# Attention, two expert layers, one kernel: another order for the last attention tiles, and all stores of x on SyncE

## The chip, the cores and the metric

One core of one Trainium2 chip. The metric is the device time of one execution in microseconds (us), and a kernel's time is the median of its runs. Engines are named as in the profile: PE (TensorE), DVE (VectorE), ACT (ScalarE), POOL (GpSimd) and SP (SyncE, which here only issues DMAs).

## The reference

Three layers, all in float32, one after the other:

```python
# q, k, v: (4, 8, 576, 64); rel = query position - key position
scores = q @ k.T / 8                       # heads 0-3 keep 0 <= rel < 32
p = softmax(mask(scores))                  # heads 4-7 keep 0 <= rel < 128, rel % 4 == 0
x = (p @ v).transpose(0, 2, 1, 3).reshape(2304, 512)

e = argmax(x @ w_gate)                     # one of 8 experts per token
s = max_softmax(x @ w_gate) * sigmoid(x @ w_output_gate)[e]
x = s * relu(x @ w1[e]) @ w2[e]            # w1: (8, 512, 1024), w2: (8, 1024, 512)

out = softplus(x @ w_in) @ w_out           # 512 -> 2048 -> 512
```

## The kernel before, in words

**Attention.** The 2304 tokens are 20 tiles, five per batch: w = 0 to 3 have 128 tokens, w = 4 has 64. Tile i is batch i // 5. A loop over i from 0 to 21 is a pipeline written out by hand: step i makes the scores and the softmax of tile i, the transposed probabilities, sums, values and the division (`normalise`, L443) of tile i - 1, and the transposed x and its copy to SBUF (`transpose_x`, `evict_x`, L497) of tile i - 2. PE, ACT, DVE and SP each run their instructions in the order in which this text gives them out; only POOL's order is made by a scheduler. Heads 0 to 3 (half 0 of x, columns 0 to 255) use V as `vP`; heads 4 to 7 (half 1) are dilated by 4, use V as `vD`, and their rows lie in the tile as 4 residues of 32 tokens: partition 32 r + m is token 4 m + r.

**Stores of x.** `normalise` writes the finished tile to `x_dram`. For tiles 0 to 13 POOL stores half 0 (L459) and, where w < 4, half 1 by an indirect DMA whose rows are listed in `xrow` (L463); for the w = 4 tiles, and for tiles 14 to 19 wholly, SP does it: one transfer for half 0 and one per residue for half 1 (L473). Behind `normalise` in SP's order stand the loads of the next batch's V (`load_v`): six transfers of three heads of vD at w = 4, earlier ones at w = 0 and 2; and q and k of the batch after that at w = 1 and 3.

**Routing.** Tiles are routed in six groups (0 to 3, 4 to 7, 8 to 10, 11 to 13, 14 to 16, 17 to 19) by a generator that is moved on one DVE instruction at a time (`pump`, or `go` in the lists below): logits on PE, a transpose of them, the argmax, a rank within the expert by small matmuls, then the place of each token. POOL scatters the places to `idx_dram`.

**The first expert's tokens.** After group 2 one expert is picked as the first (rank 0, 424 columns) and its weights are loaded. Its x is not read back token by token but gathered in four PSUM accumulators `xacc` of 128 features each. Tokens of tiles 0 to 13 are gathered by POOL (L843, four transfers of up to 128 rows) and added by matmuls with a diagonal (`mm_gathered`, L968). Tiles 14 to 19 are read back from `x_dram` (`load_late`, `ll`, L988), scaled and split in a high and a low half (`split_late`, `sp`: high on ACT L999, low on DVE L1001), and added by a matmul with a 0/1 selection (`sel_late`, `se`, L1010; `mm_late`, L1020). Tiles 14 and 19 have 64 rows each and share one such operand. Then the four accumulators are split again, high on ACT and low on DVE (`split_rank0`, L1033, L733), and the expert's matmuls begin (L900 to L902).

**What sets the order at the end of attention.** Lists of events `at(step, place, ...)`, run by `events`; what is left runs in the list `late` after the loop (L1212). At step 20 the high and low halves of tiles 15, 14 and 16 are given out before tile 19's `evict_x`; at step 21 comes one accumulator's gathered part, then the logits of tile 19.

**PSUM.** Eight banks: two for scores, one for values, five that rotate (`ps_t`) for all transposes, logits, ranks and the fourth accumulator. After attention they are given anew: two for transposes, three for the second expert matmul, three for the first.

Of the kernel before, what the change touches and what calls it, by code (L numbers as in the profile page):

```python
# [21 lines left out]
P = 128  # L22
# [20 lines left out]
def attn_moe_softplus_kernel(ctx: ExitStack, tc: tile.TileContext, q, k, v, w_gate, w_ogate, w1, w2, w_in, w_out, out, dbg=None):  # L43
# [8 lines left out]
    NW = 5  # L52
# [9 lines left out]

    x_dram = dram.tile([NT, DM], F32, name="x_dram")
    idx_dram = dram.tile([NE * NT + 512, 2], I32, name="idx_dram")
# [16 lines left out]
    tabp = const.tile([1, 1], I32, name="tabp")  # L81
    xrow = const.tile([P, NTL], I32, name="xrow")

# [38 lines left out]
    def consts2():  # L122
        nc.gpsimd.memset(upper, 1.0)
        nc.gpsimd.affine_select(upper, upper, [[1, P]], ALU.is_gt, 0.0, base=0, channel_multiplier=-1)
        nc.gpsimd.memset(ones, 1.0)
        nc.gpsimd.memset(lg, 0.0)
        nc.gpsimd.memset(cumb, 0.0)
        nc.gpsimd.iota(rev, [[-1, NE]], base=NE, channel_multiplier=0, allow_small_or_imprecise_dtypes=True)
        nc.gpsimd.iota(eidx, [[1, NE]], base=0, channel_multiplier=0, allow_small_or_imprecise_dtypes=True)
        for r in range(4):  # L130
            nc.gpsimd.iota(
                xrow[32 * r : 32 * r + 32].rearrange("p (b w) -> p b w", w=NW),
                [[2 * S, B], [2 * P, NW]], base=2 * r + 1, channel_multiplier=8,
            )

        nc.gpsimd.memset(ebase, 0.0)
        nc.gpsimd.tensor_scalar(ebase[0:1], eidx[0:1], float(NT), None, ALU.mult)
        for b in range(B):
            nc.gpsimd.iota(pair[:, NW * b : NW * b + NW, 0], [[P, NW]], base=b * S, channel_multiplier=1)
# [89 lines left out]
    ps_o = psctx.enter_context(tc.tile_pool(name="ps_o", bufs=1, space=PSUM))  # L229
    ps_t = psctx.enter_context(tc.tile_pool(name="ps_t", bufs=5, space=PSUM))  # L230

# [69 lines left out]
    def transpose_qk(b, half, ti, y):  # L301

        ps = ps_t.tile([P, 512], F32, tag="tp", name=f"pqk{b}{half}{ti}{y}")
# [133 lines left out]

    X_POOL = GROUPS[G_DRAM][1]  # L440
    x_stores = []

    def normalise(b, w):  # L443
# [12 lines left out]
        pump()  # L456
        i = NW * b + w
        eng = nc.gpsimd if i < X_POOL else nc.sync
        sts = [eng.dma_start(x_dram[t0 : t0 + nt, :256], x2[:nt, :256])]  # L459
        if i < X_POOL and w < NW - 1:  # L460

            sts.append(
                nc.gpsimd.indirect_dma_start(  # L463
                    out=x_dram.rearrange("t (h d) -> (t h) d", h=2),
                    out_offset=IndirectOffsetOnAxis(ap=xrow[:, i : i + 1], axis=0),
                    in_=x2[:, 256:],
                    in_offset=None,
                )
            )
        else:  # L470
            rows = x_dram[t0 : t0 + nt, 256:].rearrange("(m r) d -> m r d", r=4)
            for r in range(4):
                sts.append(nc.sync.dma_start(rows[:, r], x2[32 * r : 32 * r + nt // 4, 256:]))  # L473
        for k_, st in enumerate(sts):
            on_pool = i < X_POOL and (k_ == 0 or w < NW - 1)
            for e, e_pool in x_stores:
                if on_pool or e_pool:
                    tc.declare_no_dep(st.ins, e.ins, reason="no two stores of x have a row and half in common")
            x_stores.append((st, on_pool))

    def transpose_x(b, w):
        d = tl[b, w]
        x2 = d["x"].rearrange("q a h d -> q (a h d)")
        ps = ps_t.tile([P, 512], F32, tag="tp", name=f"px{b}{w}")
        for c in range(4):
# [61 lines left out]
    def route(g):  # L547
# [16 lines left out]
        cb = K["rt"].tile([P, NE], F32, tag="rcb", name=f"rcb{g}")  # L564
        posi = t2("rposi", I32)
        V.tensor_copy(lg[:, js], xT.pop(g)[:, :G4])
# [116 lines left out]
    def order():  # L683
        V = nc.vector
        pc = K["px"][0].tile([P, 512], F32, tag=K["px"][1], name="pcnt")[:, :NE]
        nc.tensor.matmul(pc, ones, cumb[:, len(GROUPS)], start=True, stop=True)

        def o3(nm):
# [4 lines left out]

        cnt, key, rank, g, r, lt, tmp, tab = o2("ocnt"), o2("okey"), o2("orank"), o3("og"), o3("or_"), o3("olt"), o3("otmp"), o2("otab", 40)
        ov = K["rt"].tile([1, NE, NT // OVW], F32, tag="oov", name="oov", bufs=1)
# [4 lines left out]
        V.memset(tab, 0.0)  # L700
        V.scalar_tensor_tensor(key, pc[0:1], float(NE), rev[0:1], ALU.mult, ALU.add)
        V.scalar_tensor_tensor(key, first[0:1], float(2 * NE * NT), key, ALU.mult, ALU.add)
        V.tensor_copy(cnt, pc[0:1])
        yield
        V.tensor_tensor(g, bce(key, NE), bc(key, NE), ALU.is_gt)
# [246 lines left out]
    def acc(c):  # L952
        pool, tag = ((ps_s, "s"), (ps_s, "s"), (ps_o, "o"), (ps_t, "tp"))[c]
        xacc[c] = pool.tile([P, 512], F32, tag=tag, name=f"xacc{c}")
# [5 lines left out]

    def mm_gathered(cs):
        for c in cs:
            if c not in xacc:
                acc0(c)
        for t in range(ntile(CAPS[0])):
            rows = min(P, CAPS[0] - P * t)
            for c in cs:
                nc.tensor.matmul(  # L968
                    xacc[c][:, P * t : P * t + rows],
                    xg[0, t][:rows, P * c : P * c + P],  # L970
                    xacc["d", t][:rows, :rows],
                    start=False,
                    stop=False,
                    skip_group_check=True,
                )

# [125 lines left out]
    at(21, 0, ("az", 0), ("az", 1))  # L1102
    at(21, 1, ("mg", 0))
    for g, (t0, t1) in enumerate(GROUPS):
# [9 lines left out]
    at(20, 2, ("sc", 0), ("sc", 1), ("sc", 2), ("sc", 3))  # L1114
    at(20, 3, ("se", 14), ("se", 15), ("sp", 15, "hl"), ("sp", 14, "h"), ("se", 16), ("sp", 16, "h"), ("ll", 18), ("ll", 19))
    at(21, 1, ("go", 5, 4), ("sp", 16, "l"), ("mg", 1), ("go", 5, 8), ("sp", 14, "l"))
    ordering = order()

    def events(i, s):
        for what, *a in EV.get((i, s), ()):  # L1120
# [12 lines left out]
            elif what == "mg":  # L1133
                mm_gathered(a)
            elif what == "ll":
# [14 lines left out]
            elif what == "sp":  # L1150
                split_late(*a)

    for i in range(n + 2):
# [55 lines left out]
    def w_lo(i, j):  # L1209
        lo_(0, j)  # L1210

    late = []  # L1212
    for c in (2, 3):
        late += [(mm_late, 15, (c,), (0,)), (mm_gathered, NL, (c,))]
    late += [(mm_late, 15, (c,), (1,)) for c in (2, 3)] + [(mm_late, 15, (c,)) for c in (0, 1)] + [(mm_late, 16, (c,)) for c in range(NC)]
    late += [(fn, i) for fn in (sel_late, split_late) for i in range(17, n)] + [(w_lo, 17, j) for j in (0, 1)]
    late += [(mm_late, 17, (c,)) for c in range(NC)]

    late += [(mm_late, i, (c,)) for i, c in ((n - 2, 0), (n - 2, 1), (n - 1, 0), (n - 1, 1), (n - 2, 2), (n - 1, 2), (n - 2, 3), (n - 1, 3))]
    while late:  # L1220
        if bg:
            pump()
        fn, i, *a = late[0]
        g = next(g for g, (t0, t1) in enumerate(GROUPS) if t0 <= i < t1)
        if fn is mm_gathered or all(e[2] != g for e in bg):
            late.pop(0)
            fn(*a) if fn is mm_gathered else fn(i, *a)
    for fn in deferred:
        fn()
    actx.close()  # L1230
# [302 lines left out]
```

## Time and profile before

| | |
|---|---|
| Median of 3 runs | 806.53 us (804.1 to 810.0) |
| Profiled execution | 803.44 us, span of its instructions 801.8 us |
| Busy: PE, DVE, ACT, POOL | 764.0, 548.5, 479.3, 119.9 us |
| Attention with its tail | to about 157 us of the span |
| Experts, then the last layer | the rest |

How to read the rows below. Times count from the start of the span. A line of a timeline gives start, duration, engine, source line, instruction, operands and how many instructions are merged (x4); in brackets stands the idle time of the engine before it and what ended that. SPq is SP's DMA issue: the time is that of the issue, not of the transfer. A DMA issue line gives a transfer's size and the median time from issue to landing. In a line of windows, 1.00 at the clock means that PE was granted its full 2.4 GHz, 0.50 means 1.2 GHz, and a value between says that the level changed within the window.

### The profile page before, as it was taken

How to read it: one execution, taken by the hardware profiler on the slowest of the kernel's cores; microseconds unless marked ns; L12 is line 12 of the kernel's file. 1: busy time of each engine (PE TensorE's matmuls, PEld its weight loads, DVE VectorE, ACT ScalarE, POOL GpSimd, SP SyncE). 2: the span in 40 equal slices, each digit the busy share in tenths (PEclk: the TensorE clock that was granted, in tenths of full speed). 3: DMA queues.
4: the chain of work that ended last, by engine and by line, in shares of the span. 5: the costliest groups of instructions: out<-in, count | busy, mean ns of one | idle time of the engine just before them, and what ended most of it. 6: DMA issues, size and time to landing. Idle time of an engine off the chain costs nothing.

```text
span 801.8 us, 15124 instructions
## 1 busy us (share of the span) xinstructions
PE 764.0 (95%) x5542; PEld 690.7 (86%) x5543; DVE 548.5 (68%) x1098; ACT 479.3 (60%) x935; POOL 119.9 (15%) x154
## 2 busy tenths in 40 slices
PE   6998886999999999999999999999999999999994
PEld 4666665898999999999989999999998999999993
DVE  6967885763667977885698877766656656656561
ACT  4776642344556666666798878655556555655551
POOL 9814343121002011100000000110000001001001
PEclk8999997799999999999999999999999999999997
DMA  9996766255789999879524211310000001001001
GB/s 236 266 248 171 147 161 150 79 184 188 239 273 292 315 304 320 294 249 306 173 80 132 78 47 41 119 40 20 1 14 27 0 1 40 1 1 40 1 1 39
DMA packets 87008, 106.60 MB, mean 133 GB/s; under 512 B 30524, under 2 KB 61500, under 8 KB 86912
## 3 DMA queue, kind: packets, MB, share of 16 engines
q1 hardware_dynamic: 75616, 86.32, 36.9%
q0 software_dynamic: 5104, 13.40, 5.2%
q10 hardware_dynamic: 6192, 5.56, 2.0%
q8 instruction: 65, 1.06, 0.6%
q14 instruction: 31, 0.25, 0.1%
HBM read 85.03 MB, written 20.37 MB: 131 GB/s over the span
## 4 chain that ended last, share of the span: by engine, by line
PE 69%; issue 8%; DVE 5%; ACT 3%; DMA 2%; POOL 0%; ACTq 0%; SPq 0%; POOLq 0%; DVEq 0%
PE pg L900 7%; PE pg L901 7%; PE pg L902 7%; PE q L1442 7%; PE q L1441 7%; PE q L1443 7%; PE py L896 3%; PE py L897 3%; PE py L898 3%; PE ph L896 3%; PE ph L898 2%; PE ph L897 2%; PE ph L900 1%; PE ph L902 1%; PE ph L901 1%
## 5 line engine op out<-in xcount | busy, mean ns | idle before, releaser
L900 PE MATMUL pg<-xhm,wh 128*128 128x384 f32 x384 | 129.5, 337 | 0.5 <-ACT l L1408 0.4
L901 PE MATMUL pg<-xlm,wh 128*128 128x384 f32 x384 | 129.6, 338 | 0.0
L902 PE MATMUL pg<-xhm,wl 128*128 128x384 f32 x384 | 129.4, 337 | 0.0
L733 DVE TENSOR_TENSOR wl<-wr,wh 128x1024 fp32r<-128x1024 f32 (+1 forms) x86 | 98.2, 1144 | 30.7 <-ACT wh L788 30.6
L1406 ACT ACTIVATE u<-pg 128x384 f32<-128x384 f32 x96 | 47.2, 492 | 116.5 <-PE pg L902 116.4
L1442 PE MATMUL q<-wl,gh 128*128 128x512 f32 x288 | 113.2, 393 | 0.0
L1441 PE MATMUL q<-wh,gh 128*128 128x512 f32 x288 | 113.0, 393 | 0.0
L1443 PE MATMUL q<-wh,gl 128*128 128x512 f32 x288 | 112.6, 391 | 0.0
L788 ACT CAST wh<-wr 128x1024 fp32r<-128x1024 f32 x74 | 77.2, 1047 | 15.1 <-ACT y L923 5.2
L1450 POOL DMA_INDIRECT out_dram<-o,perm_sb x18 | 18.1, 1004 | 435.9 <-DVE o L260 303.2
L1412 DVE TENSOR_SCALAR w<-u 128x384 f32<-128x384 f32 x68 | 24.6, 362 | 84.7 <-ACT u L1407 84.2
L900 PEld LDWEIGHTS pg<-xhm,wh 128*128 128x128 f32 x384 | 72.1, 188 | 5.0 <-ACT l L1408 1.1
L901 PEld LDWEIGHTS pg<-xlm,wh 128*128 128x128 f32 x384 | 72.0, 188 | 3.7
L902 PEld LDWEIGHTS pg<-xhm,wl 128*128 128x128 f32 x384 | 72.1, 188 | 0.0
L1414 DVE SCALAR_TENSOR_TENSOR u<-w,u 128x384 f32<-128x384 f32 x96 | 53.7, 560 | 21.6 <-ACT w L1410 19.3
L1443 PEld LDWEIGHTS q<-wh,gl 128*128 128x128 f32 x288 | 54.1, 188 | 12.3
L1441 PEld LDWEIGHTS q<-wh,gh 128*128 128x128 f32 x288 | 54.1, 188 | 8.6
L1442 PEld LDWEIGHTS q<-wl,gh 128*128 128x128 f32 x288 | 54.0, 188 | 8.2
L896 PE MATMUL ph<-xh,wh 128*128 128x392 f32 (+5 forms) x192 | 58.6, 305 | 1.6 <-ACT y L923 0.9
L1416 DVE TENSOR_TENSOR l<-l,u 128x384 f32<-128x384 f32 x96 | 53.5, 557 | 7.7 <-ACT w L1420 0.5
L896 PE MATMUL py<-hh,wh 128*128 128x312 f32 (+8 forms) x192 | 58.4, 304 | 0.0
L897 PE MATMUL py<-hl,wh 128*128 128x312 f32 (+4 forms) x192 | 57.3, 299 | 0.1
(205 smaller groups left out, 1746.3 us busy)
## 6 DMA issues: line engine op xcount, KB each, us to landing
wr<-in_moe_w_dram SPq DMA_DIRECT2D x64, 512.0 KB, 6.1
praw<-in_moe_w_out_dram SPq DMA_DIRECT2D x12, 512.0 KB, 5.8
raw<-in_q_dram SPq DMA_DIRECT2D x8, 576.0 KB, 6.9
raw<-in_k_dram SPq DMA_DIRECT2D x8, 576.0 KB
x2r<-yT_dram SPq DMA_DIRECT2D x12, 384.0 KB, 4.2
vP<-in_v_dram SPq DMA_DIRECT2D x16, 272.0 KB, 9.0
praw<-in_moe_w_in_dram SPq DMA_DIRECT2D x8, 512.0 KB
wr<-in_moe_w_in_dram SPq DMA_DIRECT2D x8, 512.0 KB, 3.3
```

The source lines that it names most:

```text
L733: e.tensor_tensor(lo, src, hi.bitcast(F32), ALU.subtract)
L788: (eng or nc.scalar.copy)(d[1], d[0])
L896: nc.tensor.matmul(ps if wide else ps[:, :cut], wh, xh if wide else xh[:, :cut], start=wide, stop=False, skip_group_check=True)
L897: nc.tensor.matmul(ps[:, :cut], wh, xl[:, :cut], start=False, stop=False, skip_group_check=True)
L900: nc.tensor.matmul(ps, wh, xh, start=(first and i == 0), stop=False)
L901: nc.tensor.matmul(ps, wh, xl, start=False, stop=False)
L902: nc.tensor.matmul(ps, wl, xh, start=False, stop=(last and i == k - 1))
L1414: nc.vector.scalar_tensor_tensor(u, w_, 1.0, u, ALU.subtract, ALU.subtract)
L1416: nc.vector.tensor_tensor(l, l, u, ALU.subtract)
L1441: nc.tensor.matmul(acc[b, t], gh[:, ts_], wh, start=(f == 0), stop=False)
L1442: nc.tensor.matmul(acc[b, t], gh[:, ts_], wl, start=False, stop=False)
L1443: nc.tensor.matmul(acc[b, t], gl[:, ts_], wh, start=False, stop=(f == NF - 1))
```

## The change

Four edits. (1) All stores of x go to SP, two transfers per tile: half 0, and half 1 with its four residues in one, by a destination seen as 4 x 32 rows. A w = 4 tile stores 128 rows of half 1, 64 of them past its own (the next tile's store follows; `x_dram` has 64 more rows at the end). `xrow` and POOL's stores go away, and with them the declarations that two stores need not wait for each other. (2) Of the five rotating banks one becomes `ps_x0`, used by the transposes of x, by two of the first batch's transposes of q and k, and at the end by the fourth accumulator. (3) The list `late` goes away. All is in the lists of step 21, and `mm_gathered` takes one gathered tile and some accumulators at a time (before: some accumulators, all four tiles). (4) The scatter of the last group (`df`), the first part of the ordering of the experts (`or`: the count matmul and three DVE instructions) and the first two weight splits (`q`) stand in the same list.

```diff
-    x_dram = dram.tile([NT, DM], F32, name="x_dram")
+    x_dram = dram.tile([NT + P - S % P, DM], F32, name="x_dram")
...
-    ps_t = psctx.enter_context(tc.tile_pool(name="ps_t", bufs=5, space=PSUM))
+    ps_x0 = psctx.enter_context(tc.tile_pool(name="ps_x0", bufs=1, space=PSUM))
+    ps_t = psctx.enter_context(tc.tile_pool(name="ps_t", bufs=4, space=PSUM))
...
-        eng = nc.gpsimd if i < X_POOL else nc.sync
-        sts = [eng.dma_start(x_dram[t0 : t0 + nt, :256], x2[:nt, :256])]
...
+        nc.sync.dma_start(x_dram[t0 : t0 + nt, :256], x2[:nt, :256])
+
+        rows = x_dram[t0 : t0 + P, 256:].rearrange("(m r) d -> r m d", r=4)
+        nc.sync.dma_start(rows, x2[:, 256:])
...
-        pool, tag = ((ps_s, "s"), (ps_s, "s"), (ps_o, "o"), (ps_t, "tp"))[c]
+        pool, tag = ((ps_s, "s"), (ps_s, "s"), (ps_o, "o"), (ps_x0, "x0"))[c]
...
-    def mm_gathered(cs):
+    def mm_gathered(t, cs):
+        rows = min(P, CAPS[0] - P * t)
...
-    at(21, 1, ("mg", 0))
...
-    at(20, 3, ("se", 14), ("se", 15), ("sp", 15, "hl"), ("sp", 14, "h"), ("se", 16), ("sp", 16, "h"), ("ll", 18), ("ll", 19))
-    at(21, 1, ("go", 5, 4), ("sp", 16, "l"), ("mg", 1), ("go", 5, 8), ("sp", 14, "l"))
+    at(20, 3, ("se", 14), ("se", 15), ("se", 16), ("ll", 18), ("ll", 19))
+    lo2, hi2 = (0, 1), (2, 3)
+    at(21, 1, ("sp", 15, "h"), ("mg", 0, lo2), ("sp", 15, "l"), ("mg", 1, lo2), ("go", 5, 3), ("ml", 15, (2,)), ("go", 5, 1))
+    at(21, 1, ("ml", 15, (3,)), ("sp", 14, "h"), ("go", 5, 8), ("ml", 15, lo2), ("mg", 2, lo2), ("go", 5, 1), ("sp", 16, "h"))
+    at(21, 1, *(("mg", t, hi2) for t in range(3)), ("go", 5, 9), ("sp", 16, "l"), ("se", 17), ("df",), ("sp", 17, "h"), ("mg", 3, (0, 1, 2, 3)))
+    at(21, 1, *(("ml", 16, (c,)) for c in range(4)), ("sp", 17, "l"), ("se", 18), *(("ml", 17, (c,)) for c in range(4)))
+    at(21, 1, ("sp", 14, "l"), ("q", 0), ("se", 19), ("sp", 18, "hl"), *(("ml", 18, (c,)) for c in range(4)))
+    at(21, 1, ("sp", 19, "hl"), ("or",), ("q", 1), *(("ml", 19, (c,)) for c in range(4)))
...
-    late = []
-    for c in (2, 3):
-        late += [(mm_late, 15, (c,), (0,)), (mm_gathered, NL, (c,))]
-    late += [(mm_late, 15, (c,), (1,)) for c in (2, 3)] + [(mm_late, 15, (c,)) for c in (0, 1)] + [(mm_late, 16, (c,)) for c in range(NC)]
-    late += [(fn, i) for fn in (sel_late, split_late) for i in range(17, n)] + [(w_lo, 17, j) for j in (0, 1)]
-    late += [(mm_late, 17, (c,)) for c in range(NC)]
```

## Rows read from the trace of the kernel before

**Rows 1.** TensorE's waits, 155 to 300 us: total us, times, longest us.

```profile
PE ph L900 <- DVE xl L733: 1.2, 1, 1.2
```

**Rows 2.** The chain of waits, 100 to 160 us: start us, us, what.

```profile
131.81 4.24 DMA xl<-x_dram
...
136.80 0.48 ACT xT L497
...
147.48 8.02 PE xacc L1020 x38
...
156.08 0.61 DVE xl L733
```

**Rows 3.** Timeline of SyncE's DMA queue, 112 to 160 us: start us, us.

```profile
129.63 2.14 SPq L473 DMA_DIRECT2D x_dram<-x  x4
131.81 0.90 SPq L988 DMA_DIRECT2D xl<-x_dram  x2
```

**Rows 4.** Groups in 131 to 157 us: busy us, mean ns | idle.

```profile
L968 PE MATMUL xacc<-diag,xg 128*128 128x128 f32 (+1 forms) x32 | 8.5, 413 | 1.7 <-DMA xg<-x_dram,idx 1.7
...
L1001 DVE SCALAR_TENSOR_TENSOR l<-xl,pair,h 128x512 fp32r<-128x512 f32 (+1 forms) x6 | 4.4, 745 | 1.5 <-ACT h L999 1.4
...
L1010 DVE TENSOR_SCALAR sel<-slots,rm 128x424 fp32r<-128x424 f32 (+1 forms) x6 | 2.4, 435 | 0.0
L733 DVE TENSOR_TENSOR wl<-wr,wh 128x1024 fp32r<-128x1024 f32 x2 | 2.4, 1222 | 0.0
L733 DVE TENSOR_TENSOR xl<-xacc,xh 128x424 fp32r<-128x424 f32 x4 | 2.3, 597 | 4.9 <-ACT xh L1033 4.9
...
L507 PE MATMUL pl<-xT,wg 128*32 128x128 f32 x8 | 1.9, 421 | 1.0 <-ACT xT L497 1.0
...
L486 PE MATMUL px<-identf,x 128*128 128x128 f32 x4 | 0.7, 286 | 0.1
```

**Rows 5.** The timeline of VectorE, 112 to 160 us: group 5's routing.

```profile
140.47 0.20 DVE L566 COPY lg<-plt 128x48 f32<-128x48 f32 x1
...
143.51 0.17 DVE L617 RECIPROCAL pair<-rs 128x3 f32<-128x3 f32 x1
```

**Rows 6.** Windows: length, busy PE PEld DVE ACT POOL, clock, DMA share, GB/s.

```profile
126.00:128.00 2.00, 0.85 (x11) 0.66 (x10) 1.80 (x11) 1.18 (x3) 1.00 (x1) 1.00 0.49 155
128.00:130.00 2.00, 2.00 (x35) 1.74 (x35) 1.31 (x9) 0.20 (x1) 1.39 (x3) 0.53 0.65 172
148.00:150.00 2.00, 2.00 (x11) 1.93 (x10) 1.51 (x3) 0.00 (x0) 0.21 (x1) 0.85 0.17 50
```

**Rows 7.** The timeline of VectorE: tiles 8, 13 and 19 normalised.

```profile
69.04 0.69 DVE L450 TENSOR_TENSOR x<-o,rc 128x512 f32<-128x512 f32 x1 [0.54 <-PE o L424]
...
99.17 0.69 DVE L450 TENSOR_TENSOR x<-o,rc 128x512 f32<-128x512 f32 x1
...
131.09 0.69 DVE L450 TENSOR_TENSOR x<-o,rc 128x512 f32<-128x512 f32 x1 [1.78 <-PE o L424]
```

**Rows 8.** The timeline of TensorE, 45 to 112 us: the dilated half's values.

```profile
78.90 0.62 PE L424 MATMUL o<-vD,pt 128*32 128x128 f32 x16
...
106.75 0.91 PE L424 MATMUL o<-vD,pt 128*32 128x128 f32 x16
```

**Rows 9.** The timeline of SyncE's DMA queue, 0 to 140 us: one V load.

```profile
66.04 0.60 SPq L284 DMA_DIRECT2D vD<-in_v_dram  x1
```

**Rows 10.** DMA issues in 20 to 160 us, KB each, median us to landing.

```profile
xl<-x_dram SPq DMA_DIRECT2D x4, 256.0 KB, 5.0
...
x_dram<-x SPq DMA_DIRECT2D x16, 32.0 KB, 2.7
```

**Rows 11.** The page: a queue (packets, MB, share), an issue (us to landing).

```profile
q1 hardware_dynamic: 75616, 86.32, 36.9%
...
vP<-in_v_dram SPq DMA_DIRECT2D x16, 272.0 KB, 9.0
```

**Rows 12.** Busy time by engine and DMA share in 72 to 80 us.

```profile
72.00:80.00 8.00, 8.00 (x160) 6.16 (x162) 5.34 (x13) 6.57 (x12) 4.43 (x5) 1.00 0.18 44
```

More of the change, by code (lines that the diff above doesn't have):

```diff
@@ L81, in attn_moe_softplus_kernel @@
     tabp = const.tile([1, 1], I32, name="tabp")
-    xrow = const.tile([P, NTL], I32, name="xrow")
     tl = {}
@@ L129, in consts2 @@
         nc.gpsimd.iota(eidx, [[1, NE]], base=0, channel_multiplier=0, allow_small_or_imprecise_dtypes=True)
[L130 to L134, printed above, removed]
         nc.gpsimd.memset(ebase, 0.0)
@@ L301, in transpose_qk @@
     def transpose_qk(b, half, ti, y):
-        ps = ps_t.tile([P, 512], F32, tag="tp", name=f"pqk{b}{half}{ti}{y}")
+        own = b == 0 and (half, ti, y) in ((0, 0, 2), (1, 0, 2))
+        ps = (ps_x0 if own else ps_t).tile([P, 512], F32, tag="x0" if own else "tp", name=f"pqk{b}{half}{ti}{y}")
         def to(t, y):
@@ L437, in sums @@
         pump()
-    X_POOL = GROUPS[G_DRAM][1]
-    x_stores = []
     def normalise(b, w):
@@ L456, in normalise @@
         pump()
-        i = NW * b + w
-        eng = nc.gpsimd if i < X_POOL else nc.sync
-        sts = [eng.dma_start(x_dram[t0 : t0 + nt, :256], x2[:nt, :256])]
[L460 to L479, printed above, removed]
+        nc.sync.dma_start(x_dram[t0 : t0 + nt, :256], x2[:nt, :256])
+        rows = x_dram[t0 : t0 + P, 256:].rearrange("(m r) d -> r m d", r=4)
+        nc.sync.dma_start(rows, x2[:, 256:])
     def transpose_x(b, w):
@@ L483, in transpose_x @@
         x2 = d["x"].rearrange("q a h d -> q (a h d)")
-        ps = ps_t.tile([P, 512], F32, tag="tp", name=f"px{b}{w}")
+        ps = ps_x0.tile([P, 512], F32, tag="x0", name=f"px{b}{w}")
         for c in range(4):
@@ L564, in route @@
         cb = K["rt"].tile([P, NE], F32, tag="rcb", name=f"rcb{g}")
-        posi = t2("rposi", I32)
+        posi = (const.tile([P, 4], I32, name="rposi_last")[:, :G4] if g == len(GROUPS) - 1 else t2("rposi", I32))
         V.tensor_copy(lg[:, js], xT.pop(g)[:, :G4])
@@ L684, in order @@
         V = nc.vector
-        pc = K["px"][0].tile([P, 512], F32, tag=K["px"][1], name="pcnt")[:, :NE]
+        pc = ps_t.tile([P, 512], F32, tag="tp", name="pcnt")[:, :NE]
         nc.tensor.matmul(pc, ones, cumb[:, len(GROUPS)], start=True, stop=True)
+        cnt, key = [const.tile([1, NE], F32, name=nm) for nm in ("ocnt", "okey")]
+        V.scalar_tensor_tensor(key, pc[0:1], float(NE), rev[0:1], ALU.mult, ALU.add)
+        V.scalar_tensor_tensor(key, first[0:1], float(2 * NE * NT), key, ALU.mult, ALU.add)
+        V.tensor_copy(cnt, pc[0:1])
+        yield
         def o3(nm):
@@ L692, in o2 @@
             return K["rt"].tile([1, n], F32, tag=nm, name=nm, bufs=1)
-        cnt, key, rank, g, r, lt, tmp, tab = o2("ocnt"), o2("okey"), o2("orank"), o3("og"), o3("or_"), o3("olt"), o3("otmp"), o2("otab", 40)
+        rank, g, r, lt, tmp, tab = o2("orank"), o3("og"), o3("or_"), o3("olt"), o3("otmp"), o2("otab", 40)
         ov = K["rt"].tile([1, NE, NT // OVW], F32, tag="oov", name="oov", bufs=1)
@@ L700, in order @@
         V.memset(tab, 0.0)
[L701 to L704, printed above, removed]
         V.tensor_tensor(g, bce(key, NE), bc(key, NE), ALU.is_gt)
@@ L964, in mm_gathered @@
                 acc0(c)
[L965 to L975, printed above, removed]
+            nc.tensor.matmul(
+                xacc[c][:, P * t : P * t + rows],
+                xg[0, t][:rows, P * c : P * c + P],
+                xacc["d", t][:rows, :rows],
+                start=False,
+                stop=False,
+                skip_group_check=True,
+            )
     def rows_of(i):
@@ L1133, in events @@
             elif what == "mg":
-                mm_gathered(a)
+                mm_gathered(*a)
+            elif what == "ml":
+                mm_late(*a)
             elif what == "ll":
@@ L1151, in events @@
                 split_late(*a)
+            elif what == "df":
+                deferred.pop()()
+            elif what == "or":
+                next(ordering)
     for i in range(n + 2):
@@ L1208, in attn_moe_softplus_kernel @@
             K["rt"] = K["rt2"]
-    def w_lo(i, j):
-        lo_(0, j)
-    late = []
-    for c in (2, 3):
-        late += [(mm_late, 15, (c,), (0,)), (mm_gathered, NL, (c,))]
-    late += [(mm_late, 15, (c,), (1,)) for c in (2, 3)] + [(mm_late, 15, (c,)) for c in (0, 1)] + [(mm_late, 16, (c,)) for c in range(NC)]
-    late += [(fn, i) for fn in (sel_late, split_late) for i in range(17, n)] + [(w_lo, 17, j) for j in (0, 1)]
-    late += [(mm_late, 17, (c,)) for c in range(NC)]
[L1219 to L1229, printed above, removed]
     actx.close()
```

## The prediction, made before the changed kernel was run

> **What bounds the kernel now.** I read the list of waits after 155 us first: TensorE waits once for the first expert matmul and hardly again [rows 1], so from there to the end the span is TensorE's work, and a microsecond saved before it is a microsecond off the span. Then the chain of waits between 131 and 157 us [rows 2], the stretch that the new tail order rewrites. The reader is to see a queue of unlike things. SyncE issues the load of tile 16's x at 131.81; it lands 4.2 us later; ScalarE makes the high half of that tile, and only then copies tile 19's transposed x (136.80). That copy had nothing to wait for: it stands behind the high half in ScalarE's order. Tile 19's logits, the last routing and everything of tiles 17 to 19 follow from it. The stretch ends with 38 accumulating matmuls in a row and the last xl split on VectorE at 156.69, for which the first expert matmul waits 1.2 us [rows 1, 2]. SyncE's queue shows why the load was late: the four half-1 stores of tile 18 stand ahead of it, 2.14 us of issue [rows 3].
>
> **The tail, part by part.** In the new order nothing of tiles 14 to 16 stands ahead of tile 19's copy. Tile 19's x is normalised at 131.8 [rows 7]; transposes 0.7 [rows 4] and copy 0.5 [rows 2] with their gaps put the logits at 133.1 instead of 137.3.
>
> VectorE from there, by the grouped rows of 131 to 157 us [rows 4]: six low halves 4.4; three of the six selections 1.2 (the other three come first, to 133.6); two weight splits 2.4; four xl splits 2.3. The routing of group 5 from its copy at 140.47 to the end of its reciprocal is 3.2, and seven small ones (two copies ahead of it, the place cast, the count's keys) at the reciprocal's 0.17 are 1.2 [rows 5]. Sum 14.7, from 133.6 to 148.3. Three times VectorE has to wait for TensorE (transposed logits, ranks, count), each behind a block of accumulating matmuls; a block of four gathered ones is 8.5 / 8 at the low clock and some 0.5 at the high one [rows 4]; three times 0.5 is 1.5, and the last xl is written at 149.8.
>
> TensorE over the same stretch: 8 logits matmuls 1.9, 32 gathered 8.5, mostly at the low clock [rows 4], so 5.2 at the high one; 38 late ones in 8.0, mostly at the high clock [rows 2]. Sum 13.1, from 133.1 to 146.2: below VectorE's 149.8, so VectorE sets the end if the clock is high. The own bank for the fourth accumulator takes away the 1.2 us wait: the expert matmuls' first bank no longer holds the accumulator that is split last. They can begin with the first split, and since four terms of three matmuls take about as long as four splits (2.3), the start in effect is some 1.7 ahead of 149.8: 148.1 against 156.7, a gain of **8.6**.
>
> The clock is the doubtful part. The granted clock was at half after a stretch in which TensorE was busy 0.85 of 2.00 us, and came back only within 148 to 150 [rows 6]. With the copy in time the one gap left near there is some 0.6 us, so I expect the high level for most of the tail. If it stays at the low one as long as before (0.85 of the level over 148 to 150 is a rise at 148.6), 15.5 us do half their work, 7.75 of 13.1, the rest ends at 154.0, the last split at 155.0, and the gain is 3.4. Bounds 3.4 and 8.6; I take **7.0**, nearer the upper, because TensorE then has nearly no idle time left there.
>
> **Loads and late tiles.** With two issues of about 0.5 each [rows 3] instead of five per tile, SyncE is out of the way 1.5 us earlier per tile; the load of tile 19 still has to wait until its store has landed, but it is used only after tile 18's halves, some 10 us after x, so it is covered. If that cover went, the exposed part would be a landing, 5.0 [rows 10]. The load also needs a free buffer, which the split of tile 15 gives at about 134.6, in time. A w = 4 tile now stores 64 rows too many, which the next tile overwrites: its half-1 store must wait for the earlier one to land. The issue behind it is a load needed 10 us later or more; costed at nothing, at most 2.7 [rows 10].
>
> **Moved from GpSimd to SyncE.** Fourteen tiles' stores leave GpSimd, which is on no link of that chain; taken as nothing. On SyncE they stand, in order, ahead of the next batch's V loads, which before were issued as soon as a buffer was free. The last six of each batch (three heads of vD) come behind the x store of the batch's fourth tile. For the second and third change that tile is normalised at 69.7 and 99.9 [rows 7]; two stores 1.0, and the sixth of six issues at 0.60 [rows 9] starts 4.0 later: 73.7, 103.9. With a landing of 5.0, the nearest row in kind (a load by SyncE in a busy stretch [rows 10]), they are there at 78.7 and 108.9; TensorE reads them at 78.9 and 106.75 [rows 8]. So the second fits by a hair, as the first does, whose code and spacing are those of the second, and the third costs 2.1. Lower bound: with the 2.7 of a small store none is late, 0. Upper bound: with 9.0, as the V loads of the first half needed, 3.8 + 3.8 + 6.1 = 13.7 [rows 11]. I take **2.1**.
>
> **PSUM and the rest.** Four rotating banks for five, with the x transposes moved out of them: no wait of TensorE in the list names such a bank, so 0; at most a bank is short once a batch by one half-clock block of transposes, 0.7 [rows 4], or 2.8 in all. Dropping the iota on GpSimd and the indirect stores: 0.
>
> **Sum.** 7.0 - 2.1 = 4.9. The profiled execution took 803.4 (span 801.8 and 1.6 around it), 3.1 under the median of 806.5; so 798.5 for such an execution, and 801.6 at the level of the median.
>
> **Rivals.** (a) **All of it comes through**: the V loads land in time and the clock stays high, 8.6 gained: 797.9. For it: the DMA engines have room just where the second batch's loads are needed [rows 12]. Against: every one of the three batches has to be in time.
>
> (b) **The order does not do what it says**: the clock stays low for the tail and the expert matmuls still wait for the last split (if a bank is held by another tile). Gain 3.4 - 1.7 = 1.7, less 2.1: 806.9. For it: before, the clock came back only in the late block, at 148 or after [rows 2, 6].
>
> (c) **Slower, the V loads behind the x stores**: TensorE waits at the first vD matmuls of tiles 5, 10 and 15 by the upper bound, 13.7, and the tail gives 7.0: 813.2. It decides from a landing of about 6.7 us on: there the waits are 1.5 + 1.5 + 3.8 = 6.8 and take nearly all that the tail gives. For it: the V loads are the longest to land in the page [rows 11]. Against: the engines were busy only 0.18 of 72 to 80 us, just where the second batch is needed [rows 12].
>
> (d) **Few queues for half 1.** Its destination is written as 4 x 32 x 256, so the outermost count is 4. If only four of the sixteen queues carried it, each would serve 32 packets of 1 KB in place of 8; at 62.6 ns a packet (36.9% of 16 x 801.8 us over 75616 packets [rows 11]) that is 2.0 instead of 0.5 us, 1.5 more per tile, and every load ends with its slowest queue. By tile 8 nine tiles have added 13.5; the idle 0.82 of 72 to 80 us gives back 6.6 [rows 12], so the V loads of the second change come 6.9 late and the rest is as forecast: 808.5. The Trainium skill, page "DMA: Bandwidth & Descriptors", section "Why a DMA increments its semaphore by 16 and not by 1", has the rule that speaks for it: the engine count is the largest number up to 16 that divides the slowest dimension of both sides, which is 4 here. No row of the kernel before has such a shape, so the trace neither bears it out nor excludes it. That the queues also lack the slack is the weaker half: the engines' busy share counts waiting packets.
>
> **Chances.** Forecast 0.50, (a) 0.24, (b) 0.10, (c) 0.08, (d) 0.08. One per cent is 8.1 us, about what a measurement of this kernel can tell from no change. Faster by more needs under 798.5: most of (a) and the best of the forecast, 0.26. Slower by more needs over 814.6: half of (c) and the far end of (d), 0.06. Within: 0.68. The range takes in (a) with the scatter of the runs, (b), (d) and the near part of (c): 795.5 to 811.
>
> **What the changed profile would show.** Right: tile 19's copy directly behind its transposes; granted clock high from there to the experts; the first expert matmul not waiting for the last split; VectorE without gaps over the last 10 us. Wrong: TensorE waiting for a V load at tile 5, 10 or 15; the half-1 store landing much later than half 0; the last late matmuls waiting for tile 19's load; the clock at half until the late block. A span above 806 would mean that the loads, not the tail, decide.

## The result, and the profile after

| | kernel before | changed kernel |
|---|---|---|
| median of 8 runs each, us | 806.2 (804.1 to 810.0) | 800.1 (796.0 to 802.0) |
| ratio, 95% interval | | 0.9915 [0.9891, 0.994] |
| profiled execution, us | 803.4 | 800.0 |
| its span, us | 801.8 | 798.4 |
| x of tile 19 normalised at | 131.09 | 137.75 |
| first expert matmul at | 156.74 | 153.62 |

The change makes the kernel 6 us faster. The two profiled executions are only 3.4 apart, because that of the kernel before lies under all 8 of its runs. Within them the two terms can be read separately: tile 19's x comes 6.7 us later, and from there to the first expert matmul (below: the tail) it is 15.9 us in place of 25.7.

The tail first. This is the chain of waits of the changed kernel (start us, us, what); [rows 2] is the same stretch of before:

```profile
137.75 0.70 DVE x L442
...
139.19 0.59 ACT xT L470
...
139.83 1.06 PE pl L480 x8
...
150.48 1.62 PE xacc L992 x7
...
152.51 1.20 DVE wl L707
153.71 0.52 DVE xl L707
...
154.27 0.46 PE ph L875
```

The copy of tile 19's transposed x (ScalarE, 139.19) stands right behind its transposes; before, it stood behind the high half of a late tile [rows 2]. The first expert matmuls no longer wait for the last split: one low half is made (153.71), and the chain goes on in the ph matmuls. The windows (length, then busy time of PE, PEld, DVE, ACT, POOL, then the granted clock, DMA share and GB/s) answer to [rows 6]:

```profile
142.00:144.00 2.00, 2.00 (x17) 1.90 (x17) 1.29 (x9) 0.22 (x1) 1.00 (x2) 1.00 0.41 138
...
148.00:150.00 2.00, 2.00 (x12) 1.72 (x10) 1.93 (x4) 0.72 (x1) 1.83 (x1) 1.00 0.13 44
```

The granted clock is 1.00 in every 2 us from 138 to 154. Before, it was 0.50 from about 135 to 148.6; these are two of the windows:

```profile
135.00:137.00 2.00, 1.30 (x4) 0.93 (x4) 0.66 (x2) 1.02 (x3) 0.96 (x1) 0.50 0.69 230
...
145.00:147.00 2.00, 2.00 (x8) 1.75 (x9) 1.97 (x3) 0.77 (x2) 0.00 (x0) 0.50 0.00 0
```

Then the front. TensorE's waits up to 155 us (total, times, longest) and VectorE's timeline at tiles 5, 15 and 19:

```profile
PE o L419 <- DMA vD<-in_v_dram: 4.2, 6, 1.6
...
PE plt L502 <- DMA vD<-in_v_dram: 1.3, 1, 1.3
```

```profile
55.48 0.69 DVE L442 TENSOR_TENSOR x<-o,rc 128x512 f32<-128x512 f32 x1 [3.24 <-PE o L419]
...
116.44 0.69 DVE L442 TENSOR_TENSOR x<-o,rc 128x512 f32<-128x512 f32 x1 [2.88 <-PE o L419]
...
137.75 0.69 DVE L442 TENSOR_TENSOR x<-o,rc 128x512 f32<-128x512 f32 x1 [0.55 <-PE o L419]
```

Tiles 5 and 15 were normalised at 52.20 and 107.70 before. So 3.3 us are lost by tile 5 (1.1 of them by tile 3, without a wait for V), 4.2 by tile 6, 5.3 by tile 10 and 8.7 by tile 15; 2.1 come back before tile 19. At tiles 5 and 15 VectorE waits for TensorE's values, and these for V. The waits for V are 5.5 us in all. Behind those at tile 5 and around those at tile 15 the granted clock is 0.50 as well, from 56 to 58 us and from 114 to 120, where it was 1.00 before; tile 6 loses its 0.9 there. SyncE's queue at the third batch (start us, us), and the chain's link at the same place:

```profile
105.46 0.32 SPq L449 DMA_DIRECT2D x_dram<-x  x1
105.84 0.55 SPq L452 DMA_DIRECT2D x_dram<-x  x1
106.44 0.87 SPq L278 DMA_DIRECT2D vD<-in_v_dram  x1
...
109.94 0.59 SPq L282 DMA_DIRECT2D vD<-in_v_dram  x1
...
118.48 0.38 SPq L449 DMA_DIRECT2D x_dram<-x  x1
124.28 0.54 SPq L452 DMA_DIRECT2D x_dram<-x  x1
```

```profile
109.30 6.30 DMA vD<-in_v_dram
```

The two x stores at 105.46 could not go before tile 13 was normalised (104.75), the six V loads stand behind them, the last is issued at 109.94, and one of them takes 6.3 us to land.

### The profile page after: what moved, and what is told of

Same layout as the page of the kernel before. It is cut to its first block, busy times and chain, and to the rows that moved or that the text cites. A ratio compares the mean times of both kernels' runs of the same rounds, so it can differ in the third digit from the quotient of the medians.

```text
span 798.4 us, 15087 instructions
## 1 busy us (share of the span) xinstructions
PE 761.2 (95%) x5542; PEld 689.2 (86%) x5543; DVE 545.8 (68%) x1098; ACT 478.5 (60%) x935; POOL 100.3 (13%) x124
## 4 chain that ended last, share of the span: by engine, by line
PE 71%; issue 8%; DVE 4%; ACT 3%; DMA 2%; POOL 0%; ACTq 0%; SPq 0%; POOLq 0%
PE pg L874 7%; PE pg L875 7%; PE pg L876 7%; PE q L1404 7%; PE q L1403 7%; PE q L1405 7%; PE ph L870 3%; PE py L870 3%; PE py L871 3%; PE ph L872 3%; PE ph L871 3%; PE py L872 3%; PE ph L874 1%; PE ph L875 1%; PE ph L876 1%
## 5 line engine op out<-in xcount | busy, mean ns | idle before, releaser
L1412 POOL DMA_INDIRECT out_dram<-o,perm_sb x18 | 18.5, 1026 | 434.1 <-DVE o L254 301.4
L1376 DVE SCALAR_TENSOR_TENSOR u<-w,u 128x384 f32<-128x384 f32 x96 | 53.7, 559 | 21.6 <-ACT w L1372 19.3
```

The lines of the kernel that those rows point to most:

```text
L1376: nc.vector.scalar_tensor_tensor(u, w_, 1.0, u, ALU.subtract, ALU.subtract)
```

## The experiments

They were timed in three groups, each against runs of the kernel before made with it. In the first and second group the kernel before took 817.6 and 816.0 us, in the third 806.9, as with the result above. The expectations call this a property of the chip; it is not, since the second and third group ran on the same chip. What is known of the higher level is told last. Times are compared within a group only. "Order theory", "bank theory" and the like are the names that the expectations give to their readings.

| group | kernel | median us | before | ratio, 95% interval |
|---|---|---|---|---|
| 1 | tail order alone | 814.4 | 817.6 | 0.9947 [0.9927, 0.9968] |
| 1 | stores alone | 815.5 | 817.6 | 0.9976 [0.9953, 0.9999] |
| 1 | loads ahead of stores | 808.6 | 817.6 | 0.9887 [0.9865, 0.9909] |
| 1 | and spread over four steps | 805.9 | 817.6 | 0.9854 [0.9829, 0.9879] |
| 2 | before itself | 816.9 | 816.0 | 1.0009 [0.998, 1.0039] |
| 2 | changed kernel | 807.1 | 816.0 | 0.9906 [0.9874, 0.9938] |
| 2 | shared bank | 811.5 | 816.0 | 0.9961 [0.9939, 0.9983] |
| 2 | splits first | 811.2 | 816.0 | 0.9941 [0.9917, 0.9965] |
| 3 | changed kernel | 800.9 | 806.9 | 0.9930 [0.9909, 0.9950] |
| 3 | loads ahead, spread | 794.1 | 806.9 | 0.9852 [0.9831, 0.9874] |
| 3 | half 0 as 4 x 32 (turned out to be the changed kernel) | 802.6 | 806.9 | 0.9943 [0.9922, 0.9964] |
| 3 | scatter twice | 807.4 | 806.9 | 1.0003 [0.9987, 1.0019] |

### Group 1: the two parts alone, and the loads moved

**Tail order alone.** The changed kernel with the old stores:

```
...
-        nc.sync.dma_start(x_dram[t0 : t0 + nt, :256], x2[:nt, :256])
...
-        rows = x_dram[t0 : t0 + P, 256:].rearrange("(m r) d -> r m d", r=4)
-        nc.sync.dma_start(rows, x2[:, 256:])
+        i = NW * b + w
+        eng = nc.gpsimd if i < X_POOL else nc.sync
+        sts = [eng.dma_start(x_dram[t0 : t0 + nt, :256], x2[:nt, :256])]
...
```

> The changed kernel with the stores of x as before (GpSimd to tile 13, SyncE in five transfers from tile 14, the rest of a batch in four). Order theory (the tail gives some 9 us, the stores on SyncE ahead of the V loads cost 6 to 7 before tile 19): x of tile 19 is normalised at about 131 as before, the first expert matmul starts some 16 us behind it, at about 147.5, and the time is about 9 us under the kernel before, 797. Bank theory (the loss before tile 19 comes from four rotating PSUM banks in place of five): tile 19 is normalised at 137 to 138 here too and the time is that of the changed kernel, 800. Third reading (the short tail needs the two-transfer stores, because tile 19's load comes later behind four residue stores): tile 19 at 131, but the first expert matmul only 19 us or more behind it, 800 to 801.

It is 4.3 us faster than the kernel before (0.9947), where the order theory said 9. The tail is as short as it said: the first expert matmul comes 16.3 us behind tile 19's x. So the order shortens the tail without the two-transfer stores, and the third reading falls. Tile 19's x stands at 152.95 in its trace, but that can't be compared, since this group has no trace of the kernel before, and by its time alone the run does not part the order theory from the bank theory. Why the gain is only half is seen in the second group.

**Stores alone.** The kernel before with the new stores:

```
...
-        eng = nc.gpsimd if i < X_POOL else nc.sync
...
+        nc.sync.dma_start(x_dram[t0 : t0 + nt, :256], x2[:nt, :256])
...
+        rows = x_dram[t0 : t0 + P, 256:].rearrange("(m r) d -> r m d", r=4)
+        nc.sync.dma_start(rows, x2[:, 256:])
```

> The kernel before with nothing but the new stores (two transfers per tile by SyncE, none by GpSimd). Order theory: TensorE waits for vD and vP at tiles 5, 10 and 15, x of tile 19 is normalised at 137 to 138, and the time is 6 to 7 us over the kernel before: 812 to 813. Bank theory: no such waits, tile 19 at 131, 806. If the two-transfer stores also help the old tail (tile 16 to 18 loaded earlier), 1 to 2 us less than the order theory's number.

The order theory missed: no loss of 6 to 7 us, rather 2 less than before. The waits for V are nearly gone here (total us, times, longest):

```profile
PE o L417 <- DMA vD<-in_v_dram: 0.4, 1, 0.4
```

TensorE stands still for 7.6 us of this trace with nothing to wait for. That the late loads land in that time is the likely reading; it was not tested by itself.

**Loads ahead of the stores**, and then also **spread over four steps**. In both, nothing but the order of SyncE's instructions changes (the loads of q and k move with those of V):

```
             values(*tiles[i - 1])
+        if i < n and b + 1 < B:
+            for half, heads in (((0, (0, 1)),), (), ((0, (2, 3)), (1, (0,))), (), ((1, (1, 2, 3)),))[w]:
+                load_v(b + 1, half, heads)
+            if w in (1, 3) and b + 2 < B:
+                load_qk(b + 2, w // 2)
+        if 1 <= i < n + 1:
             normalise(*tiles[i - 1])
-        if i < n and b + 1 < B:
...
```

```
-(((0, (0, 1)),), (), ((0, (2, 3)), (1, (0,))), (), ((1, (1, 2, 3)),))[w]
+(((0, (0, 1)),), ((0, (2, 3)),), ((1, (0, 1)),), ((1, (2, 3)),), ())[w]
```

> The changed kernel with the V loads and the q and k loads of a tile step issued just ahead of the x stores of that step, in place of just behind them; nothing else moves. Order theory (the loads are late because they stand behind stores that wait for x): each load moves ahead by nearly one tile, some 5 us, the waits at tiles 5, 10 and 15 (2.2, 1.1 and 3.3) go, x of tile 19 is normalised at 132 to 134, and the time is 4 to 6 under the changed kernel: 794 to 796. Queue theory (half 1 runs on few DMA queues and so all transfers land late) or traffic theory (DMA engines lack room): the waits stay for the most part, 799 to 800.

> As the run before it, and the V loads are spread over the first four tile steps of a batch (half 0 in steps 0 and 1, half 1 in steps 2 and 3, none in step 4), so the last of them leave one more tile ahead. Order theory: no wait for V is left; at most 1 us under the run with the loads ahead of the stores, 793 to 796. Traffic theory: 799 to 800, and the waits only move to other tiles.

9.2 and 11.9 us under the kernel before by the ratios; the changed kernel itself, at the same level in the next group, is 7.7 under it. So the first gives 1.5 where 4 to 6 were expected, and the second 4.2, with intervals that overlap. TensorE's waits for V are 0.5 us in the first trace and none in the second, as the order theory said; but at this level few were left to win.

### Group 2: both kernels at the higher level, the bank and the splits

**The kernel before and the changed kernel once more.**

> The kernel before itself, for a profile on the chip of this call. The first four runs took place on a chip on which the kernel before took 817.55, 11 more than in the first profile, and in their traces TensorE sits idle for 5.5 to 8.1 us between 20 and 140 us with nothing that the profile shows to wait for ("issue"), against 1.4 and 0.7 in the two first profiles. Chip theory (these gaps belong to the chip, whatever the kernel): on a chip where this kernel takes 815 or more its trace shows 5 to 8 us of such gaps, on one where it takes 806 it shows under 2. Edit theory (the gaps come with the edits): under 2 on either.

> The changed kernel itself, for a profile beside that of the kernel before on one chip. Order theory: first expert matmul 16 to 18 us behind tile 19's x (the kernel before: 25 to 26), tile 19's x 5 to 7 later than in the kernel before, time 6 to 7 under it. If the two terms come out otherwise on one and the same chip, the terms read from the first two profiles were in part the scatter of an execution.

Here tile 19's x comes at 146.30 before and at 144.88 after, not later but 1.4 earlier; the first expert matmul is 20.7 and 15.9 us behind it. The changed kernel gains 7.7 (0.9906), as at the lower level, yet out of other terms. Both traces show the idle time that hides the late loads. TensorE's waits for nothing, of before:

```profile
PE s L368 <- issue: 3.4, 4, 1.0
...
PE pl L507 <- issue: 2.0, 5, 0.5
...
PE o L424 <- issue: 0.7, 2, 0.4
```

and of the changed kernel:

```profile
PE s L363 <- issue: 3.3, 6, 1.0
...
PE o L419 <- issue: 2.0, 3, 1.3
...
PE o L419 <- DMA vD<-in_v_dram: 1.4, 2, 1.2
```

With 5.3 us of these gaps only 1.4 us of waits for V are left, against 5.5 in the first trace. So far the chip theory's numbers hold (6.3 in the kernel before here, 1.4 in its first trace), though "chip" is the wrong name. The old tail is 4.9 shorter than in the first profile, and the clock is the likely reason (windows of the kernel before, its tail from 146.3 on):

```profile
146.00:148.00 2.00, 2.00 (x12) 1.08 (x11) 1.66 (x9) 0.39 (x1) 0.09 (x1) 0.67 0.04 13
...
154.00:156.00 2.00, 2.00 (x12) 1.76 (x9) 1.97 (x12) 0.58 (x2) 0.00 (x0) 0.54 0.10 8
156.00:158.00 2.00, 2.00 (x10) 1.78 (x10) 1.95 (x4) 1.68 (x3) 0.00 (x0) 0.61 0.00 0
158.00:160.00 2.00, 2.00 (x11) 1.89 (x12) 1.93 (x3) 0.00 (x0) 0.76 (x8) 1.00 0.00 0
```

A mean of 0.54 or 0.61 over 2 us is 1.8 or 1.6 us at half the clock, and up to 1.3 more lie behind 146.3: 3.4 to 4.7 us, in place of some 13.7. If TensorE set the pace all through, the 9 to 10.3 us between them did half their work at half the clock, 4.5 to 5.2 us: by this estimate the whole difference. It was not tested by itself. So read, the gain of the first pair of profiles was won in good part from an old tail that ran at the low clock.

**The shared bank**: the x transposes and the fourth accumulator come from five rotating banks again.

```
...
-        ps = ps_x0.tile([P, 512], F32, tag="x0", name=f"px{b}{w}")
+        ps = ps_t.tile([P, 512], F32, tag="tp", name=f"px{b}{w}")
...
-        pool, tag = ((ps_s, "s"), (ps_s, "s"), (ps_o, "o"), (ps_x0, "x0"))[c]
+        pool, tag = ((ps_s, "s"), (ps_s, "s"), (ps_o, "o"), (ps_t, "tp"))[c]
```

> The changed kernel with five rotating banks as before: the x transposes and the fourth accumulator come from the rotation, no bank of its own. Own-bank step (worth 1.2 to 1.7): the first expert matmul waits for the last xl split again by 1.2, and the time is 1 to 2 over the changed kernel. Bank theory (four rotating banks cost time in attention): tile 19's x comes 3 us or more earlier than in the changed kernel and the time is under it. If the bank does neither: within 1 of the changed kernel.

It is slower than the changed kernel by 4.5 us of the ratios (0.9961 and 0.9906; one interval ends at 0.9938, the other begins at 0.9939). TensorE waits for the last xl split again:

```profile
PE ph L873 <- DVE xl L706: 2.0, 1, 2.0
```

That is 2.0 in place of 0.3: the own bank is worth 1.7, the forecast's figure. The tail is 19.5 against 15.9; the rest fits the clock, which is 0.67 from 144 to 146 and 0.50 from 146 to 148, behind 2 us (142 to 144) in which TensorE was busy for 0.36. The bank theory falls: tile 19's x is 2.0 earlier, under the 3 that it asked for (in the next run, with four rotating banks, it is 2.3 earlier too), and the time is longer.

**The splits first**: late tiles 15, 14 and 16 are split ahead of tile 19's transposes again.

```
...
-    at(20, 3, ("se", 14), ("se", 15), ("se", 16), ("ll", 18), ("ll", 19))
+    at(20, 3, ("se", 14), ("se", 15), ("sp", 15, "hl"), ("sp", 14, "h"), ("se", 16), ("sp", 16, "h"), ("ll", 18), ("ll", 19))
...
```

> The changed kernel with the splits of late tiles 15, 14 (high half) and 16 (high half) put back ahead of tile 19's transposes, as before; the rest of the new order stays. Order theory: ScalarE's copy of tile 19's transposed x waits behind tile 16's high half again, which waits for its load, so the logits of tile 19 come some 4 us later, the clock falls in the gap, and the first expert matmul is 20 us or more behind tile 19's x (4 over the changed kernel). Rival (the late load is in time now, since SyncE has two stores per tile ahead of it in place of five): within 1.5 of the changed kernel.

By the ratios 2.9 slower than the changed kernel (the intervals overlap), between the two numbers expected; the tail is 19.0, 3.2 longer. ScalarE's timeline:

```profile
143.87 1.95 ACT L971 ACTIVATE h<-xl,pair 128x512 fp32r<-128x512 f32 x3 [5.92 <-issue]
145.72 0.56 ACT L470 COPY xT<-px 128x512 f32<-128x512 f32 x1
```

The three high halves stand ahead of the copy and hold it until 145.72, some 1.3 after the transposes; they start with the weights that VectorE writes at 143.65, not with a load, so the 4 us of the order theory are not there. The clock is 0.50 from 144 to 148, but TensorE also stood still for 3.5 us ahead of these transposes with nothing to wait for. How the 3.2 divide between the order and that gap stays open, and 2.9 is not far over the 1.7 by which two series of one program differ in the third group.

### Group 3: at the level of the result

> The changed kernel itself, as reference on the chip of this call. On a chip where the kernel before takes 806: 6 under it, with 5 us of waits for V loads before tile 19. On one where it takes 815 or more: 6 to 8 under it, with under 2 us of such waits, since gaps of another cause (5 to 6 us of TensorE idle with nothing to wait for) cover the late loads.

> The kernel with the V loads ahead of the x stores and spread over four tile steps, once more, beside the changed kernel on one chip. Order theory: no wait for V; on a chip of the 806 kind 5 to 7 under the changed kernel (its late loads cost 6.7 there), on one of the 816 kind 2 to 4 under it (11.9 under the kernel before, against 7.7). Rival (the order of loads and stores is worth nothing, and the difference between the two earlier calls is one of chips): within 1 of the changed kernel.

The changed kernel is 6.0 under the kernel before by medians. With the loads ahead and spread it is 12.8 under it and 6.8 under the changed kernel, with intervals apart. TensorE's waits for V in the changed kernel of this group:

```profile
PE o L419 <- DMA vD<-in_v_dram: 5.6, 5, 1.9
...
PE plt L502 <- DMA vD<-in_v_dram: 1.2, 1, 1.2
```

The list of the other kernel has no load of V in it, and tiles 5 and 19 are back in time:

```profile
52.57 0.69 DVE L442 TENSOR_TENSOR x<-o,rc 128x512 f32<-128x512 f32 x1 [1.02 <-DMA x_dram<-x]
...
130.41 0.69 DVE L442 TENSOR_TENSOR x<-o,rc 128x512 f32<-128x512 f32 x1 [0.62 <-PE o L419]
```

130.41 against 131.09 before [rows 7] and 137.15 in the changed kernel of this group: 6.74 us come back by nothing but the place of the loads of V, q and k in SyncE's order. Its first expert matmul is at 146.32, 15.9 behind tile 19's x. This version beats both kernels. The rival falls.

**Half 0 written like half 1**, as 4 x 32 x 256:

```
-        nc.sync.dma_start(x_dram[t0 : t0 + nt, :256], x2[:nt, :256])
+        nc.sync.dma_start(x_dram[t0 : t0 + nt, :256].rearrange("(r m) d -> r m d", m=32), x2[:nt, :256])
```

> The changed kernel with half 0 of x written in the same way as half 1, its destination as 4 x 32 x 256 (the rows and the bytes are the same). Queue theory (the four as the outermost count puts a store on 4 of the 16 queues, 1.5 us more per tile): the suspect is doubled, V loads come another 1.5 us later per tile, the waits for them grow by 4 us or more and the time by 4 to 7; half 0 takes as long to land as half 1. Order theory: the time is that of the changed kernel within 1.

This edit changes nothing. The four blocks of 32 rows lie one behind the other in `x_dram`, so the destination folds back to 128 rows of 256, and the two programs are the same instruction for instruction. The traces agree: SyncE takes 0.37 us (median of 20) to issue half 0 here and 0.38 in the changed kernel, and 0.56 to issue half 1 in both. So the queue theory was not tested. What the run gives is the scatter of one program: 1.7 us between the medians of two series (with intervals that overlap), and 4.5 us in tile 19's x, at 141.60 here and at 137.15 there. Most of that is lost at the second batch, where the profile puts a single long wait down to a load of the other half of V:

```profile
PE o L419 <- DMA vP<-in_v_dram: 4.7, 1, 4.7
...
PE o L419 <- DMA vD<-in_v_dram: 2.7, 3, 1.5
```

**The scatters of the first three groups twice**, into a second table that is not read:

```
...
+        if g < G_DRAM:
+            for w in range(t1 - t0):
...
+                sc = nc.gpsimd.indirect_dma_start(
+                    out=idx2_dram[:, :],
...
```

> The changed kernel with the GpSimd scatters of places and weights of the first three groups (11 indirect transfers of 8-byte elements) issued a second time into a table that nobody reads. Burst theory (the gaps in attention on the chips of the 816 kind, and the late third batch of V on the first chip, come with these bursts, in which TensorE, VectorE or loads stand still): x of tile 19 comes 4 us or more later and the time is 4 to 8 over the changed kernel. Rival (the bursts only happen to lie there): within 1 of the changed kernel, since GpSimd has over 20 us of idle time between 77 and 102.

6.4 over the changed kernel by medians: the burst theory's number. Its sign is there too, tile 19's x at 144.93, 7.8 later than in the changed kernel of this group, but this profiled execution is 5 over its kernel's median, and 4.2 of the 7.8 are lost by tile 8 (75.59 against 71.35), before any doubled transfer. From tile 8 to tile 14 attention takes 37.3 us, and 37.5 in the changed kernel. The other 3.7 come behind tile 14, and two things are late there. SyncE's half-1 store of tile 15 stands still for 13.2 us (6.1 in the changed kernel) until that of tile 14, issued at 123.12, has landed:

```profile
123.12 0.62 SPq L453 DMA_DIRECT2D x_dram<-x  x1
...
137.57 0.54 SPq L453 DMA_DIRECT2D x_dram<-x  x1
```

And GpSimd, which gave out doubled transfers up to 123, waits 7.0 us for its places to land and gathers the first expert's rows at 144.36 against 135.02. VectorE waits 3.3 us for those places, read back, ahead of tile 19's x, and TensorE for the rows:

```profile
PE xacc L953 <- DMA xg<-x_dram,idx: 2.8, 1, 2.8
```

The clock then falls to 0.50 and the tail is 21.6. So the doubled transfers may have held up a store and the gather; one late execution does not show it. Of the gaps of the higher level TensorE has 0.7 us here; what they come with was not settled.

## Why the forecast was right, and where it was not

The sum was right: 4.9 forecast, 6.0 measured, inside the range; the interval of the first ratio is 4.8 to 8.8 us, that of the third group 4.0 to 7.3. Both of its terms were too small, though, and that their errors nearly cancelled was luck.

**The tail, 7.0 forecast, 9.8 in the first pair of profiles** (25.7 to 15.9), over the upper bound of 8.6. The mechanism was right in its main steps: the copy behind its transposes, the clock high, and at the end VectorE's splits ahead of the expert matmuls. The failing step was the choice of 7.0 between the bounds for a clock that might stay low. In all four traces of the changed kernel it stayed at 1.00 through the tail (in that of the second group from 146 on), and then the forecast's own way of counting gives 8.6. The doubt was not idle: with the loads ahead in the first group the clock fell, and the tail took 18.4 and 18.5. Of the other 1.2, 0.7 is that the last split ends 17.3 us after tile 19's x is written where 18.0 was worked out, and 0.4 that the first expert matmul stands 2.1 ahead of that, not 1.7. The tail is also the term that hangs most on the execution: 17.5 in the changed kernel of the third group, where TensorE waited 1.9 for gathered rows, and from the higher level's old tail of 20.7 there were only 4.9 to win. At the lower level there is one trace of the old tail. (The forecast's sum for TensorE, 5.2 and 8.0, is 13.2 and not 13.1; nothing hangs on it.)

**The own bank, 1.7**: 2.0 of waiting against 0.3, right.

**V loads, 2.1 forecast, 6.7 in the profiles**, 6.74 when they are moved ahead; in the other two traces of the changed kernel at this level tile 19's x came 6.1 and 10.5 after that of the kernel before. This is the step that failed, in two places. The first is the landing: 5.0 was called the nearest row in kind, but the list of DMA issues of the kernel before has a row for these loads themselves, and one for a store of half 1's size:

```profile
vD<-in_v_dram SPq DMA_DIRECT2D x16, 192.0 KB, 7.7
...
x_dram<-x SPq DMA_DIRECT2D x4, 128.0 KB, 5.8
```

With 7.7 the forecast's own sum, the first batch taken as the second, loses 2.5 + 2.5 + 4.9 = 9.9 us, more than the 7.0 of the tail, and its sign would have been wrong. In the third batch the load on the chain took 6.3; with that the sum gives 1.1 + 1.1 + 3.5 = 5.7, and TensorE's waits for V were 5.5.

The second is "The first fits as its code and spacing are those of the second", which did not hold. SyncE's own waits at 47 to 52 us (total, times, longest) show what the sum left out:

```profile
SPq L278 <- DMA raw<-in_q_dram: 1.9, 1, 1.9
SPq L282 <- DMA raw<-in_k_dram: 1.2, 1, 1.2
```

The six issues were counted at 0.60 each, with nothing between them. In the first batch the last two of them stood still for 1.9 and 1.2 us until the loads of q and k issued at 42.51 and 43.02 had landed, and TensorE waited 1.8 for them at tile 5. No data joins these loads. They stand eight places apart in SyncE's order, and the program has eight counters for the completion of such transfers, taken in turn, so that nearly every issue waits until the one eight places ahead has landed. The two stores per tile that came to SyncE use up such places. The second batch, forecast to fit by a hair, lost 1.1 at tile 10, and the third 3.3 where 2.1 was forecast; the low clock behind the waits is in no term either.

Rival (c) named the mechanism, with 6.8 us of waiting from a landing of 6.7 on. It came near that: 5.5 of waiting at a landing of 6.3 and 6.7 lost by tile 19, divided otherwise among the batches, and only the larger gain of the tail kept the sign.

**PSUM, 0**: not contradicted; with five banks again the time was longer, not shorter.

**Late tiles and the longer store, 0**: right in time, wrong in size. Tile 15's half-1 store waited 5.3 us for that of tile 14 to land (SyncE's rows at 118.48 and 124.28), where at most 2.7 was given, the row of a 32 KB store (the row of a 128 KB store above says 5.8). Nothing behind it was needed soon in the result; in the run with the doubled scatters the same store waited 13.2.

**Rivals.** (a), everything comes through, was shown to be possible by the version with the loads ahead, 12.8 us under the kernel before by medians, more than the 8.6 it was priced at. (b) fell: one split ahead of the experts and the high clock. (d) is not borne out at its price of 808.5: the result and the faster version with the loads ahead both have half 1 in that shape. Tile 14's half-1 store landed 6.5 us after its issue (117.76 to 124.28), little over the 5.8 of the half-0 stores that SyncE made before. The run that was to double the suspect did not, so no experiment isolates the shape. The Trainium skill, page "DMA: Bandwidth & Descriptors", section "Why a DMA increments its semaphore by 16 and not by 1", has the rule behind (d); no view here shows on how many engines a store ran, so the rule itself is neither shown nor refuted.

## What to carry to other kernels

A store that waits for a result holds everything that is issued behind it on the same engine: put loads that wait for nothing ahead of it in program order; here that was worth more (6.8 us) than the change under study (6.0). When loads are moved behind something, count the queue's own waits for earlier transfers, and take the landing from the row of that very load: the trace before had 7.7 where 5.0 was used. An edit of a transfer's shape can fold away; look whether its issue time has moved. And a gain in a stretch whose clock is low is a gain on that clock: ask how long the old stretch would stay low in another execution.

## What the runs showed of the hardware that was not expected

**Two levels of one kernel.** The kernel before took 806 to 807 us in two sessions and 816 to 818 in two others, one of each on the same chip. In all eight traces of the higher level TensorE is idle for 5.3 to 9.5 us between 20 and 150 us with nothing that the profile names, in the six of the lower level for 0 to 1.4 (in two of these six ScalarE has one such stop, of 4.4 and 6.2 us, and in one VectorE, of 3.2, all between 111 and 119 us). At the higher level VectorE and ScalarE often stand still in the same places. In the kernel before one such place is 75 to 79 us, where VectorE stands still for 4.25 us and TensorE gives out one to three matmuls at a time:

```profile
76.23 0.27 PE L507 MATMUL pl<-xT,wg 128*32 128x128 f32 x1 [0.30 <-issue]
76.95 0.39 PE L507 MATMUL pl<-xT,wg 128*32 128x128 f32 x3 [0.45 <-issue]
77.66 0.27 PE L507 MATMUL pl<-xT,wg 128*32 128x128 f32 x1 [0.32 <-issue]
```

What the engines lack there is open. The Trainium skill, page "Runtime: NRT & Kernel Launch", section "Instruction fetch mechanics", says that code is fetched in blocks by the engine's own queue and that this is mostly hidden; no run here tells whether a late block is the cause.

**The clock in the tail.** Where the new order ran at 1.00 from 138 us or earlier, and nothing was late, the tail took 15.9 us (the result, and the loads ahead in the third group). With the same loads in the first group the clock is 0.50 from 142 to 148 us, behind 2 us (140 to 142) in which TensorE does nothing, and the tail took 18.5.
